# Eight weight-remainder subtractions moved from VectorE to GpSimd in a sparse-attention and feed-forward kernel

## The chip, the cores and the metric

The kernel runs on one core of one Trainium2 chip. A core has five engines with instruction queues of their own, which run in order: PE (TensorE, matrix products), DVE (VectorE), ACT (ScalarE), POOL (GpSimd) and SP (here it only issues transfers). The metric is the device time of one execution in microseconds, lower is better; the median of three runs stands for the kernel.

## The reference

Attention over 8 batches and 8 heads of 576 tokens with two kinds of masks, then a feed-forward layer over all 4608 tokens. Cut to what matters:

```python
scores = where(mask, q @ k.T / 8, -1e9)      # 4 heads local (32 back), 4 heads strided by 32
x = (softmax(scores) @ v)                    # then laid out as [4608, 512]
h = x @ w_in                                 # w_in  [512, 2048]
g = where(h >= 1, h, where(h <= -1, 0, (h + 1) ** 2 / 4))
out = g @ w_out                              # w_out [2048, 512]
```

The two weight matrices are given in double precision; everything else is single precision.

## The kernel before, in words

**Products.** Each single-precision factor is held as two parts in the matmul's input format `float32r`: a rounded high part and a low part, the remainder. A product is three matmuls (high by high, high by low, low by high; `HI_LO`). The last one of each three needs the low part of the weights.

**Chunks.** The 4608 tokens are cut in chunks of 512. Chunks 0 to 2 (`CLASSIC`) go through the feed-forward layer directly: for each of 16 blocks f of 128 hidden units, `up(c, f)` makes h (12 matmuls, line 775), the activation runs on ACT and DVE (lines 779, 782, 785), `rounded` splits it into `gh` and `gl` (lines 803 to 806), and two blocks later `down(c, f)` adds to the output (12 matmuls, line 820). The h tile of block f shares its bank with block f+2, so `up(c, f+2)` also waits for `gl` of block f. The remaining chunks use sums of weight blocks that POOL forms (`combine`, lines 396 and 398) and that go through DRAM.

**Weights.** In the first chunk the weights are not ready: block f arrives as raw 64-bit words, half 0 being `w_in` and half 1 `w_out`, and is turned into high and low parts while PE already works on the first blocks. A step is written as a letter, the block and the half, so `E4.0` is the low part of block 4's `w_in`:

- `A` (ACT, line 343) and `L` (ACT, line 347) scale the two 32-bit words of each number, `B` (DVE, line 351) shifts the high word, `C` (POOL, line 355) adds the two words. Now the number is single precision.
- `D` (ACT, line 364) rounds it to the high part, `E` (DVE, line 368) subtracts that from it and stores the low part. Both write the tile `w_f`.

`up(0, f)` needs `D` and `E` of half 0, `down(0, f)` those of half 1. When the last `E` of a block is done, its raw tile is free, and `stage()` loads another block into the place through SP's queue.

**Order.** All instructions stand in an order written out by hand: tables of numbers (`WORK`, `CONV`, ...) give each step a place on a common axis, on which a block of chunk 0 takes 4 units, from -64 to 0; the steps are sorted by that number, and each engine runs its own in that order. `CONV` holds the weight steps. Between them stand the steps of attention for the next batch: on POOL the subtraction of the row maximum (line 572) and the scaling by the row sum (line 596), on ACT the exponential (line 579), on DVE the masks, maxima and sums (lines 542, 568, 583). An engine that waits for one step's input holds up everything behind it in its queue.

Of the kernel before, what the change touches and what calls it, by code (L numbers as in the profile page):

```python
# [8 lines left out]
F32 = mybir.dt.float32  # L9
# [4 lines left out]
ALU = mybir.AluOpType  # L14
# [95 lines left out]
     (337.09, 3), (339.07, 6), (347.97, 4)]}  # L110

CONV = [(-63.99, 'L0.1'), (-63.97, 'A0.1 B0.1'), (-63.52, 'A1.1'), (-63.03, 'C0.1'), (-62.58, 'A3.0'), (-62.43, 'D0.1'),
# [28 lines left out]
G_WORK = {0: [(165.99, 's11'), (167.56, 's10'), (183.93, 's12'), (187.61, 's20'), (187.74, 's13'), (188.3, 't60'),  # L141
# [32 lines left out]
def tile_sparse_attention_then_ffn(  # L174
# [14 lines left out]
    nc = tc.nc  # L189
# [119 lines left out]
    def place(u, shape, dtype, name):  # L309
        return slot(f"w{u}", shape, dtype, name)  # L310
# [20 lines left out]
    def words(f, i):  # L331

        if i == 2:
            yield raws[f].rearrange("p i e t -> p (i e) t"), f in wt and wt[f].rearrange("p i h x e -> p (i h) x e")
            return
        for raw, e in pieces[f, i]:
            yield raw, f in wt and wt[f][:, i, e.start // HF:e.stop // HF]
# [19 lines left out]
    def whole(raw):  # L357
        return raw[:, :, 1].bitcast(F32).rearrange("p (h e) -> p h e", e=HF)

    def conv_d(f, i, copy=nc.scalar.copy):  # L360
        if f not in wt:
            wt[f] = place(f, [P, 2, 2, 2, HF], F32R, f"w_{f}")
        for raw, to in words(f, i):
            copy(to[:, :, 0], whole(raw))

    def conv_e(f, i):
        for raw, to in words(f, i):
            nc.vector.tensor_tensor(out=to[:, :, 1], in0=whole(raw), in1=to[:, :, 0].bitcast(F32), op=ALU.subtract)
        if i and f < len(PLACES):
            held.discard(PLACES[f])  # L370

# [2 lines left out]
    def stage(n=len(PLACES)):  # L374
        nonlocal staged
        while staged < n and ((staged, 0) in pieces or PLACES[staged] not in held):
            if (staged, 0) not in pieces:
                load_w(staged, 0)
            load_w(staged, 1)
            staged += 1  # L380
# [611 lines left out]
    def down_block(s, between):  # L992
        home = {"y": ("b0", "b1"), "x": ("b2", "b3"), "z": ("b4", "b5")}
        for n, (m, k) in enumerate(DOWN):
# [20 lines left out]


    conv = {"A": conv_a, "L": conv_l, "B": conv_b, "C": conv_c, "D": conv_d, "E": conv_e,
            "G": lambda f, i: conv_d(f, i, nc.vector.tensor_copy)}

    def begin(names):  # L1020
        for name in names.split():
# [6 lines left out]

    def conv_step(name):
        conv[name[0]](*map(int, name[1:].split(".")))  # L1030
        if name[0] == "E":
            stage()

    def last_weights(n):
# [8 lines left out]
    with tc.manual_schedule():  # L1043
# [33 lines left out]
        for s, work in G_WORK.items():  # L1077
            for t, name in work:
# [3 lines left out]
                agenda.append((t, 4, do, what))  # L1082
        agenda += [(t, 3, ship, (f, i)) for i, ts in enumerate(SHIP) for f, t in enumerate(ts)]
        agenda += [(t, 5, conv_step, (name,)) for t, names in CONV for name in names.split()]
        agenda.sort(key=lambda a: a[:2])

# [89 lines left out]
```

## Time and profile before

| | |
|---|---|
| median of 3 runs | 815.0 us (814.41, 815.0, 818.4) |
| profiled execution | 817.29 us, its span 815.5 us |
| granted TensorE clock | 1.00 |
| busy, share of the span | PE 99%, DVE 70%, ACT 61%, POOL 29% |

The span reaches from the first to the last instruction of the profiled execution; the 1.8 us between it and that execution's own time lie outside the program's instructions. Rows of the timeline give start and length in us, the engine, the line of the program, the operation, the tile written and those read, the shapes, how many like instructions were put together (`x2`), and in brackets how long the engine had been idle and what ended that. `fp32r` is the matmul input format. Instructions of one engine overlap by up to 0.1 us in the records, since one starts while the last still drains.

### The profile page before, as it was taken

To read this page: it belongs to the slowest core of one execution; us is meant where nothing else is said; L and a number is where in the kernel's file an instruction comes from. 1 tells how busy PE (TensorE), PEld (TensorE's weight loads), DVE (VectorE), ACT (ScalarE), POOL (GpSimd) and SP (SyncE) were. 2 spreads that over 40 slices of the span, in tenths; PEclk is the share of its full clock that TensorE was granted. 3 is DMA by queue.
4 is the path that set the end of the run, shared out by engine and by line. 5 is a ranking of instruction groups with operands and counts; after the bars stand their busy time and mean duration, and the time that the engine had idled before them with its cause. 6 is when DMAs were issued, how large, how long until landed. Compare 5 with 4: busy or idle time off the path is not lost.

```text
span 815.5 us, 17861 instructions
## 1 busy us (share of the span) xinstructions
PE 806.2 (99%) x6969; PEld 656.9 (81%) x6969; DVE 574.7 (70%) x850; ACT 495.4 (61%) x866; POOL 232.5 (29%) x226
## 2 busy tenths in 40 slices
PE   8999999999999999999999999999999999999998
PEld 6788888878878888887878888888888888888886
DVE  5898868767548477776778876675589834558664
ACT  5888955545355365776775453778654647775442
POOL 5353544873347543023222000220120001114100
PEclk9999999999999999999999999999999999999999
DMA  9936437788868867987998768887666776666765
GB/s 344 408 138 201 153 111 274 265 298 278 265 221 299 286 243 257 304 287 247 285 288 266 216 203 249 263 265 228 193 193 213 232 235 196 196 192 190 216 200 170
DMA packets 101796, 195.10 MB, mean 239 GB/s; under 512 B 17105, under 2 KB 32465, under 8 KB 99665
## 3 DMA queue, kind: packets, MB, share of 16 engines
q1 hardware_dynamic: 92496, 164.60, 63.3%
q10 hardware_dynamic: 9216, 29.36, 9.4%
q8 instruction: 55, 0.90, 0.5%
q14 instruction: 29, 0.23, 0.1%
HBM read 147.26 MB, written 46.66 MB: 238 GB/s over the span
## 4 chain that ended last, share of the span: by engine, by line
PE 91%; DMA 5%; issue 1%; DVE 1%; ACT 1%; POOL 0%; SPq 0%; ACTq 0%; POOLq 0%
PE o L820 16%; PE h L775 16%; PE yo L1005 15%; PE y L917 15%; PE zo L1005 8%; PE z L917 7%; PE xo L1005 4%; PE x L917 4%; PE xp L669 3%; PE sc L482 3%; DMA wr<-kq 1%; DMA qk<-in_qk_s 1%; DMA there<-t 1%; DMA pT<-there 1%; DMA qk<-in_qk_l 1%
## 5 line engine op out<-in xcount | busy, mean ns | idle before, releaser
L917 PE MATMUL y<-x,wr 128*128 128x512 f32 x576 | 141.3, 392 | 0.0
L775 PE MATMUL h<-xq,w 128*128 128x512 f32 x576 | 140.0, 392 | 0.1
L1005 PE MATMUL yo<-hl,wr 128*128 128x512 f32 x576 | 132.8, 390 | 0.6 <-DMA wr<-kq 0.6
L820 PE MATMUL o<-gh,w 128*128 128x512 f32 x384 | 130.1, 399 | 0.0
L1005 PEld LDWEIGHTS yo<-hl,wr 128*128 128x128 f32 x576 | 108.0, 188 | 23.4 <-DMA wr<-kq 1.0
L775 PEld LDWEIGHTS h<-xq,w 128*128 128x128 f32 x576 | 107.4, 188 | 23.4 <-DVE xq L739 0.7
L917 PEld LDWEIGHTS y<-x,wr 128*128 128x128 f32 x576 | 107.4, 188 | 22.7
L820 PEld LDWEIGHTS o<-gh,w 128*128 128x128 f32 x384 | 72.1, 188 | 16.2
L820 PE MATMUL o<-gl,w 128*128 128x512 f32 x192 | 75.0, 391 | 0.0
L917 PE MATMUL z<-x,wr 128*128 128x512 f32 x288 | 73.7, 391 | 0.0
L957 POOL TENSOR_TENSOR ga<-gb,ga 128x1024 f32<-128x1024 f32 x9 | 21.6, 2397 | 167.5 <-DVE ga L785 141.7
L1005 PE MATMUL zo<-hl,wr 128*128 128x512 f32 x288 | 66.1, 390 | 0.0
L572 POOL TENSOR_TENSOR pr<-pr,st 128x384 f32<-128x384 f32 (+3 forms) x21 | 26.3, 1253 | 135.7 <-DVE st L595 64.5
L1005 PEld LDWEIGHTS zo<-hl,wr 128*128 128x128 f32 x288 | 54.0, 188 | 11.3
L917 PEld LDWEIGHTS z<-x,wr 128*128 128x128 f32 x288 | 53.8, 188 | 11.3
L782 ACT ACTIVATE tmp<-tmp 128x512 f32<-128x512 f32 x96 | 60.7, 632 | 3.0
L871 DVE TENSOR_TENSOR hl<-ga,hl 128x1024 fp32r<-128x1024 f32 x36 | 47.3, 1315 | 19.9 <-ACT hl L870 18.2
L870 ACT CAST hl<-ga 128x1024 fp32r<-128x1024 f32 x36 | 38.0, 1056 | 35.1 <-PE yo L1005 12.6
L396 POOL TENSOR_TENSOR xs<-w 128x512 f32<-128x512 f32 x32 | 45.1, 1426 | 48.4 <-DMA ks<-xs 32.8
L785 DVE SCALAR_TENSOR_TENSOR h<-h,u 128x512 f32<-128x512 f32 x47 | 32.8, 697 | 30.5 <-ACT u L782 30.1
L398 POOL TENSOR_TENSOR xs<-xs 128x256 f32<-128x256 f32 x64 | 51.3, 802 | 5.0
L779 ACT ACTIVATE u<-h,half 128x512 f32<-128x512 f32 x48 | 33.1, 689 | 29.6 <-PE h L775 24.1
(120 smaller groups left out, 1321.9 us busy)
## 6 DMA issues: line engine op xcount, KB each, us to landing
wr<-ks SPq DMA_DIRECT2D x192, 256.0 KB, 3.9
wr<-kq SPq DMA_DIRECT2D x144, 256.0 KB, 3.4
ks<-xs ACTq DMA_DIRECT2D x16, 1024.0 KB, 4.8
raw<-in_w SPq DMA_DIRECT2D x30, 512.0 KB, 9.6
kq<-w ACTq DMA_DIRECT2D x48, 256.0 KB, 3.8
qk<-in_qk_s SPq DMA_DIRECT2D x16, 604.0 KB, 6.1
qk<-in_qk_l SPq DMA_DIRECT2D x16, 576.0 KB, 6.0
v<-in_v_l SPq DMA_DIRECT2D x21, 384.0 KB, 6.0
```

What stands on the lines that cost most here:

```text
L396: nc.gpsimd.tensor_tensor(out=b[:, :, f] if i else b[:, f], in0=hi, in1=lo, op=ALU.add)
L398: nc.gpsimd.tensor_tensor(out=st[:, to, HF:], in0=st[:, x, HF:], in1=st[:, y, HF:], op=op)
L572: eng.tensor_tensor(out=pr, in0=pr, in1=st[:, 0].unsqueeze(2).broadcast_to(list(pr.shape)), op=ALU.add)
L775: nc.tensor.matmul(o_ps[c, f], wt[f][:, 0, h, x, e:e + P], xq[c][:, y, cc], start=first and n == 0, stop=last and n == len(todo) - 1)
L779: nc.scalar.activation(u, h, AF.Relu, bias=half, scale=0.5)
L782: nc.scalar.activation(u, u, AF.Square)
L785: nc.vector.scalar_tensor_tensor(out=to, in0=h, scalar=1.0, in1=u, op0=ALU.max, op1=ALU.min)
L820: nc.tensor.matmul(o_ps[c][d], wt[f][:, 1, h, x, e:e + P], gs[y], start=f == 0 and n == 0, stop=f == NF - 1 and n == 2)
L870: nc.scalar.copy(t[:, 0], src)
L871: nc.vector.tensor_tensor(out=t[:, 1], in0=src, in1=t[:, 0].bitcast(F32), op=ALU.subtract)
L917: nc.tensor.matmul(to, w_[:, a, c * P:(c + 1) * P], xc[m][:, b, c], start=m in (1, 2, 5) and c + q == 0, stop=c == 1 and q == 2, skip_grou ...
L1005: nc.tensor.matmul(to, w_[jj][:, a, d * P:(d + 1) * P], t[:, b, jj], start=m in (1, 2, 5) and k + jj + q == 0, stop=k == NP // 2 - 1 and j ...
```

## The change

A new step letter `N` does what `E` does, with POOL's subtraction in place of DVE's. It stands in for `E` at the same numbers in half 1 (`w_out`) of the even blocks: `N0.1`, `N2.1`, ... `N14.1`, eight steps of one instruction each, 128x512 elements. Nothing else is moved.

```diff
- (-60.82, 'E0.1'), (-60.23, 'B1.1'), (-59.82, 'L3.0'), (-59.81, 'B3.0'), (-59.68, 'C3.0'), (-59.64, 'L1.1'),
+ (-60.82, 'N0.1'), (-60.23, 'B1.1'), (-59.82, 'L3.0'), (-59.81, 'B3.0'), (-59.68, 'C3.0'), (-59.64, 'L1.1'),
...
-    def conv_e(f, i):
+    def conv_e(f, i, eng=nc.vector):
         for raw, to in words(f, i):
-            nc.vector.tensor_tensor(out=to[:, :, 1], in0=whole(raw), in1=to[:, :, 0].bitcast(F32), op=ALU.subtract)
+            eng.tensor_tensor(out=to[:, :, 1], in0=whole(raw), in1=to[:, :, 0].bitcast(F32), op=ALU.subtract)
...
-            "G": lambda f, i: conv_d(f, i, nc.vector.tensor_copy)}
+            "G": lambda f, i: conv_d(f, i, nc.vector.tensor_copy),
+            "N": lambda f, i: conv_e(f, i, nc.gpsimd)}
...
-        if name[0] == "E":
+        if name[0] in "EN":
             stage()
```

In the rows below a tile's name ends in a running number, and the number before it is the block: `raw_3_209` is the raw tile of block 3, `w_2_660` the weights of block 2; `pr_1_0` are the scores of batch 1, unit 0.

POOL's queue at the first two moved steps (line 355 is `C`; the first `raw_0` row is `C0.1`, then come `C3.0`, `C1.1`, `C2.1`, `C4.0`):

```order
 L355 TENSOR_TENSOR raw_2_204<-raw_2_204 128x512
 L355 TENSOR_TENSOR raw_0_191<-raw_0_191 128x512
+L368 TENSOR_TENSOR w_0_516<-raw_0_191,w_0_516 128x2x256
 L355 TENSOR_TENSOR raw_3_209<-raw_3_209 128x512
 L355 TENSOR_TENSOR raw_1_198<-raw_1_198 128x512
 L355 TENSOR_TENSOR raw_2_204<-raw_2_204 128x512
+L368 TENSOR_TENSOR w_2_660<-raw_2_204,w_2_660 128x2x256
 L355 TENSOR_TENSOR raw_4_216<-raw_4_216 128x512
 L572 TENSOR_TENSOR pr_1_0_812<-pr_1_0_812,st_1_0_813 128x768
```

`C3.0` and `C4.0`, the additions for the `w_in` halves of blocks 3 and 4, now stand behind `N0.1` and `N2.1`, which wait for `D0.1` and `D2.1` on ACT.

DVE's queue at the first of them, between the split of block 0's activation and the shifts `B1.1` and `B3.0`:

```order
 L805 CAST gh_0_0_707<-u_0_0_699 128x512
 L806 TENSOR_TENSOR gl_0_0_708<-u_0_0_699,gh_0_0_707 128x512
-L368 TENSOR_TENSOR w_0_516<-raw_0_191,w_0_516 128x2x256
 L351 TENSOR_SCALAR raw_1_198<-raw_1_198 128x512
 L351 TENSOR_SCALAR raw_3_209<-raw_3_209 128x512
```

DVE goes from the split straight to the shifts, one instruction of line 368 fewer.

POOL's queue at the two moved steps of blocks 6 and 8:

```order
 L355 TENSOR_TENSOR raw_6_712<-raw_6_712 128x512
 L572 TENSOR_TENSOR pr_1_2_1098<-pr_1_2_1098,st_1_2_1099 128x12x54
+L368 TENSOR_TENSOR w_6_968<-raw_6_712,w_6_968 128x2x256
 L355 TENSOR_TENSOR raw_9_721<-raw_9_721 128x512
 L355 TENSOR_TENSOR raw_8_718<-raw_8_718 128x512
+L368 TENSOR_TENSOR w_8_1107<-raw_8_718,w_8_1107 128x2x256
 L355 TENSOR_TENSOR raw_9_721<-raw_9_721 128x512
```

Here the additions `C9.0` and `C9.1` come behind the moved steps.

14 rows, old and new, of the table CONV are left out of this document.

## The prediction

> **What bounds the kernel now.** I began with the page's busy line and the chain that ended last, then the busy time in ten-microsecond stretches, then PE's waits, and last the timeline of the 30 us in which PE runs just behind its weights.
>
> ```profile
> PE 806.2 (99%) x6969; PEld 656.9 (81%) x6969; DVE 574.7 (70%) x850; ACT 495.4 (61%) x866; POOL 232.5 (29%) x226
> ...
> PE 91%; DMA 5%; issue 1%; DVE 1%; ACT 1%; POOL 0%; SPq 0%; ACTq 0%; POOLq 0%
> ```
> ```profile
> core 0: us, PE busy (x) PEld busy (x) DVE busy (x) ACT busy (x) POOL busy (x), PEclk, DMA share, GB/s
> ...
> 40.00:50.00 10.00, 10.00 (x89) 8.04 (x71) 9.74 (x20) 9.12 (x18) 5.85 (x5) 1.00 0.78 312
> 50.00:60.00 10.00, 10.00 (x92) 8.15 (x91) 9.86 (x20) 8.59 (x16) 5.02 (x6) 1.00 0.01 2
> ```
> ```profile
> PE yo L1005 <- DMA wr<-kq: 0.6, 1, 0.6
> ```
> ```profile
> PEld h L775 <- DVE w L368: 0.3, 1, 0.3
> ```
>
> PE is busy 99% of the span and makes 91% of the last chain. From 30 us on PE's matrix rows show one wait, 0.6 us, far behind the change. So relief of another engine can win almost nothing, and any time that the change makes PE wait is added whole, since nothing behind it gives it back. But the second table shows that the margin is thin where the change sits: DVE is 97 to 99% busy from 40 to 60 us, ACT 86 to 91%, and the one weight load that waited for an `E` (0.3 us, last row) shows that PE is fed just in time there. POOL, half busy, looks as if it had room; yet what counts is which steps queue behind each `N` on POOL.
>
> **Prices.** DVE's rows around the first two moved steps, `E0.1` first, then `B1.1` with `B3.0`, `E4.0`, a row sum of attention and `E5.0`:
>
> ```profile
> 31.72 0.68 DVE L368 TENSOR_TENSOR w<-raw,w 128x512 fp32r<-128x512 f32 x1
> 32.33 0.76 DVE L351 TENSOR_SCALAR raw<-raw 128x512 uint32<-128x512 uint32 x2
> ...
> 42.04 0.68 DVE L368 TENSOR_TENSOR w<-raw,w 128x512 fp32r<-128x512 f32 x1
> ...
> 43.31 0.95 DVE L583 TENSOR_REDUCE st<-pr 128x12 f32<-128x768 f32 x1
> ...
> 48.63 0.63 DVE L368 TENSOR_TENSOR w<-raw,w 128x512 fp32r<-128x512 f32 x1
> ```
>
> What goes: eight DVE instructions of line 368 of 0.68 us. The next starts 0.61 us after the first of these rows, so about 0.6 us each, 4.8 us in all on DVE. What comes: eight POOL subtractions of 128x512 with two inputs in SBUF. POOL's nearest rows:
>
> ```profile
> 115.72 2.54 POOL L396 TENSOR_TENSOR xs<-w 128x512 f32<-128x512 f32 x2 [5.83 <-PE h L775]
> ```
> ```profile
> L957 POOL TENSOR_TENSOR ga<-gb,ga 128x1024 f32<-128x1024 f32 x9 | 21.6, 2397 | 167.5 <-DVE ga L785 141.7
> ```
> ```profile
> L355 POOL TENSOR_TENSOR raw<-raw 128x512 uint32<-128x512 uint32 x16 | 17.1, 1074 | 25.4 <-DVE raw L351 10.3 <-issue 4.8 <-DMA raw<-in_w 3.8
> ```
>
> The nearest is line 396: same engine, size, two inputs, the same weight tiles, 1.27 us each. The integer `C` (1.07 us) is the low end. No row of POOL writes `fp32r`; if that halves its rate, the high end is the 2.40 us of twice as many elements on line 957. I take 1.27.
>
> **One engine holds the other.** Two pairs of rows show that POOL and some DVE operations exclude each other:
>
> ```profile
> 48.86 1.73 POOL L596 TENSOR_TENSOR pr<-pr,st 128x768 f32<-128x768 f32 x1 [1.33 <-DVE st L595]
> 49.18 1.69 DVE L351 TENSOR_SCALAR raw<-raw 128x512 uint32<-128x512 uint32 x1
> ```
> ```profile
> 59.69 2.49 POOL L355 TENSOR_TENSOR raw<-raw 128x512 uint32<-128x512 uint32 x2 [1.37 <-ACT raw L347]
> ```
> ```profile
> 59.73 1.55 DVE L368 TENSOR_TENSOR w<-raw,w 128x512 fp32r<-128x512 f32 x1
> ```
>
> At 49.18 a `B`, of which two took 0.76 us above, takes 1.69 and ends 0.3 us after POOL's instruction (50.59); at 59.73 an `E`, above 0.68, takes 1.55 beside a `C`. So an `N` holds back any `B`, `E` or scaling (line 596) that DVE reaches meanwhile, up to 1.27 us. Operations that read a bank of PSUM are not held.
>
> The Trainium skill has this as a rule (SBUF — State Buffer, section Who interferes with whom): whichever of the two engines starts first keeps the shared port pair for its whole instruction, and the other blocks. By that rule, the trace agrees: the 1.69 us. Were the engines independent, `N0.1` would end at 32.9 us, before `C3.0` is due, and the sum below would be 0.4 us smaller in its first term and 0.6 smaller in the later ones, 1.4 us in place of 2.4.
>
> **The replay from 30 to 52 us.** With DVE's rows above, those of ACT, POOL and PE:
>
> ```profile
> 30.93 0.67 ACT L364 CAST w<-raw 128x512 fp32r<-128x512 f32 x1
> ...
> 34.45 0.66 ACT L364 CAST w<-raw 128x512 fp32r<-128x512 f32 x1
> ...
> 38.84 0.67 ACT L364 CAST w<-raw 128x512 fp32r<-128x512 f32 x1 [0.23 <-POOL raw L355]
> ...
> 40.54 0.68 ACT L364 CAST w<-raw 128x512 fp32r<-128x512 f32 x1
> ...
> 42.21 0.88 ACT L579 ACTIVATE pr<-pr 128x768 f32<-128x768 f32 x1
> ```
> ```profile
> 33.22 2.04 POOL L355 TENSOR_TENSOR raw<-raw 128x512 uint32<-128x512 uint32 x2 [3.23 <-DMA raw<-in_w]
> 37.76 2.04 POOL L355 TENSOR_TENSOR raw<-raw 128x512 uint32<-128x512 uint32 x2 [2.51 <-ACT raw L347]
> 40.34 1.79 POOL L572 TENSOR_TENSOR pr<-pr,st 128x768 f32<-128x768 f32 x1 [0.54 <-DMA raw<-in_w]
> ```
> ```profile
> 43.35 2.88 PE L775 MATMUL h<-xq,w 128*128 128x512 f32 x12
> ...
> 48.79 3.09 PE L775 MATMUL h<-xq,w 128*128 128x512 f32 x12
> ```
> ```profile
> 49.31 2.14 PEld L775 LDWEIGHTS h<-xq,w 128*128 128x128 f32 x10 [0.34 <-DVE w L368]
> ```
>
> *N0.1.* `D0.1` (30.93) ends at 31.60, `N0.1` runs from 31.65 to 32.9. `E0.1` (31.72) is gone, so `B1.1` and `B3.0` (32.33, 0.76 us together) come up at 31.72 and are held until 32.9, or go first and hold `N0.1`. Either way `N0.1` and both shifts are done at 33.6 to 33.75 and `C3.0` starts then, not at 33.22: +0.5. It ends at 34.75, and `D3.0` (34.45) starts at 34.85: +0.4, which ACT's queue and the shifts carry to `D2.1` (38.84), now at 39.25. PE doesn't wait yet.
>
> *N2.1.* It waits for `D2.1` to end at 39.9 and runs to 41.2. `C4.0`, the second of the pair at 37.76, so at 38.76 before, starts only then: +2.5, and ends at 42.3. Behind it on POOL the maximum's subtraction (40.34) runs from 42.3 to about 43.8. On ACT `D4.0` (40.54) goes to 42.35; it holds ACT's queue, the exponential (42.21) started 1.7 us after it with two steps between, so now at 44.05: +1.85. Its sum on DVE (43.31) follows at 45.1: +1.8. DVE is packed from there to `E5.0`, so that goes from 48.63 to 50.4 and ends at 51.05. PE's third weight load of `up(0,5)` already waited for it (49.31) and now gets it 1.8 us later. On the way `E4.0` (42.04), held by the subtraction on POOL until 43.8, ends at 44.5, and the third matmul of `up(0,4)`, due 0.46 us after 43.35, loses 0.7 us; that is part of the 1.8, as both are counted against the same clock. DVE's saved 0.6 us each of `E0.1` and `E2.1` win nothing: DVE waits for the `D`s, exponentials and shifts that now come later.
>
> The two steps together: **1.8 us**, 0.4 from `N0.1` and 1.4 from `N2.1`.
>
> **The other six.**
>
> ```profile
> 53.72 0.56 DVE L596 TENSOR_TENSOR pr<-pr,st 128x384 f32<-128x384 f32 x1
> ...
> 54.53 1.29 DVE L368 TENSOR_TENSOR w<-raw,w 128x512 fp32r<-128x512 f32 x2
> ...
> 71.85 0.68 DVE L368 TENSOR_TENSOR w<-raw,w 128x512 fp32r<-128x512 f32 x1
> ...
> 73.17 0.69 DVE L806 TENSOR_TENSOR gl<-h,gh 128x512 fp32r<-128x512 f32 x1
> ...
> 113.25 0.69 DVE L806 TENSOR_TENSOR gl<-h,gh 128x512 fp32r<-128x512 f32 x1
> ```
> ```profile
> 55.29 2.72 PE h L775 x12
> ...
> 74.81 2.72 PE h L775 x12
> ...
> 118.36 2.72 PE h L775 x12
> ```
>
> `N4.1` falls on the scaling at 53.72 and holds it some 0.7 us; `E6.0` is the first of the pair behind it (54.53, ended 55.2) and was needed 0.46 us after `up(0,6)` began at 55.3 or a little sooner: 0.4 to 0.5 us of room against 0.7. **0.3 us.** Then the missing `E4.1` gives DVE 0.6 back. `N6.1` holds `E8.0` about as long as the missing `E6.1` had taken: 0. `N8.1` falls on `E9.0` (71.85) and pushes it and the split of block 7 (73.17, ended 73.86) by up to 1.0 us, with 0.9 us of room to `up(0,9)` at 74.81, which shares the bank: **0.3 us** with the little that DVE is behind by then. `N10.1` and `N12.1` are of the same kind (at most 1.0 less the 0.6 saved), in a stretch where the load on DVE falls. `N14.1` holds the last two `C` by up to 2.7 us and through them ACT's queue, but block 14's split (ended 113.94) is needed at 118.36: 4.4 us of room. 0. Transfers of later blocks wait for a block's last `E`; `stage()` after `N6.1` issues 0.6 us later, after `N8.1` not later than before: 0.
>
> The sum is 1.8 + 0.3 + 0.3 = **2.4 us**. The profiled execution took 817.29 us with a span of 815.5 us, so it becomes 819.7 with a span of 817.9. The median of the runs is 2.3 us below that execution, and the same 2.4 us on it give **817.4 us**.
>
> **Rivals.**
>
> *Hidden.* If `N` costs 1.07 us and POOL and DVE happen to miss each other, `C4.0` is late by 1.9 instead of 2.5, and the packed stretch behind it takes some of that from the 1.2 us of DVE time saved ahead of it. Then PE waits 0 to 0.8 us: 815.0 to 815.8. The 0.34 us wait at 49.31 speaks against it: there is no room left at that place. Chance 0.25.
>
> *Slower, by a slow `fp32r` write on POOL.* If `N` takes 2.40 us as on line 957, the 1.13 us more are added at `N0.1`, `N2.1` and `N4.1`, each with the packed chain behind it: 2.4 + 3.4 = 5.8 us, 820.8 us. It decides from the point at which the three add 1.7 us, an `N` of 1.85 us. For it: no row of POOL writes that type. Against it: DVE writes it at the same 0.68 us as `f32`. Chance 0.18.
>
> *Faster, by DVE's relief.* 4.8 us leave an engine that is 98% busy around the place. But PE is the bound and shows only 0.3 us of waiting for `E`: 814.7 us at best, so over 0.5% (4.1 us) would need PE to wait in a way these rows don't show. Chance 0.04.
>
> That the change does nothing is excluded: the order shows eight instructions on another engine.
>
> **How the numbers follow.** My forecast, a loss of 0.8 to 4.1 us, has 0.53. A measurement of this kernel tells about 0.5% from no change, 4.1 us. The forecast and the hidden case lie within that: 0.78; slower 0.18; faster 0.04. The likeliest time is 817.4 us. The range starts at 814.6, the best of the hidden case with the 0.3 us gained, and ends at 820.2, within the slow case: about 0.1 is left out above and a little below.
>
> **What would show it.** Right: line 368 on POOL near 1.27 us; `C4.0` on POOL starting near 41.3; the exponential of 42.21 near 44; PE's loads of line 775 waiting for line 368 some 2 us in all between 43 and 58 us; nothing on PE after 80. Wrong: no PE wait there (hidden), or `N` rows of 1.85 us and more. Also wrong, if PE waits in a later place, such as block 14's bank, or if a transfer that starts after an `N` arrives late.

## Result and the profile after

| | before | after | ratio (95%) |
|---|---|---|---|
| median of 10 and 10 executions | 817.37 us | 821.79 us | 1.0054 (1.0036 to 1.0073) |
| the same kernels once more, 19 and 8 | 817.53 us | 820.85 us | 1.0042 (1.0026 to 1.0058) |
| profiled execution, its span | 817.29, 815.5 us | 820.3, 818.3 us | |

The change costs 3.3 to 4.4 us, 0.4 to 0.5%; the forecast was a loss of 2.4 us, 817.4 us. The page of the changed kernel begins:

```profile
PE 808.9 (99%) x6969; PEld 657.6 (80%) x6969; DVE 575.3 (70%) x842; ACT 496.6 (61%) x866; POOL 242.8 (30%) x234
```

DVE has eight instructions fewer and POOL eight more, as forecast. DVE's busy time isn't lower for it: other instructions got longer by what was saved. PE's waits from 30 us on, where before there was one of 0.6 us far behind the change (columns: us in total, times, longest):

```profile
PE h L775 <- DVE w L368: 1.1, 2, 0.6
PE h L775 <- DVE gl L806: 0.5, 1, 0.5
PE h L775 <- ACT raw L343: 0.3, 1, 0.3
PE xp L669 <- DMA pT<-there: 0.2, 1, 0.2
```

Two waits for an `E`, one for a `gl` (the bank shared with the block two before), one whose releaser is named from ACT, and one of 0.2 us for a transfer, far behind the change (between 400 and 600 us). To weigh such waits free of what happens before and behind, the measure from here on is the **stretch**: from PE's first matmul of `up(0,2)` to its first of `up(1,0)`. Its two ends before and then after, from the timeline (between those of before stand the starts of `up(0,6)` and `up(0,9)`):

```profile
31.37 0.50 PE L775 MATMUL h<-xq,w 128*128 128x512 f32 x1
...
55.13 2.88 PE L775 MATMUL h<-xq,w 128*128 128x512 f32 x12
...
74.65 1.52 PE L775 MATMUL h<-xq,w 128*128 128x512 f32 x6
...
118.20 1.07 PE L775 MATMUL h<-xq,w 128*128 128x512 f32 x4
```
```profile
32.56 0.72 PE L775 MATMUL h<-xq,w 128*128 128x512 f32 x2
...
122.69 1.52 PE L775 MATMUL h<-xq,w 128*128 128x512 f32 x6
```

That is 86.83 and 90.13 us: 3.30 us more. (All of this profiled execution is 1.19 us late already at 32.56, ahead of the first moved step, `N0.1`.) The places, from the starts of the `up` groups:

```profile
44.59 0.73 PE L775 MATMUL h<-xq,w 128*128 128x512 f32 x2
45.89 2.56 PE L775 MATMUL h<-xq,w 128*128 128x512 f32 x10 [0.57 <-DVE w L368]
...
51.45 0.70 PE L775 MATMUL h<-xq,w 128*128 128x512 f32 x2 [0.28 <-ACT raw L343]
52.64 2.60 PE L775 MATMUL h<-xq,w 128*128 128x512 f32 x10 [0.49 <-DVE w L368]
...
58.50 3.25 PE L775 MATMUL h<-xq,w 128*128 128x512 f32 x12
...
79.01 1.17 PE L775 MATMUL h<-xq,w 128*128 128x512 f32 x4 [0.46 <-DVE gl L806]
```

`up(0,4)` breaks after its second matmul (`E4.0` is late), `up(0,5)` starts late and breaks at the same point (`E5.0`): from `up(0,2)` to `up(0,6)` it is now 58.50 - 32.56 = 25.94 us, before 55.13 - 31.37 = 23.76: **+2.18**. `up(0,6)` takes 3.25 us in place of 2.88: **+0.38** to the next block. `up(0,9)` waits for its bank: **+0.74** with what follows it. Behind that nothing until `up(1,0)`. The late start of `up(0,5)` is another wait for the bank: it comes 0.15 us after the split of block 3 ended (DVE's row at 50.61 below), as that of `up(0,9)` comes 0.15 us after the split of block 7 (78.17); the row that names ACT is most likely this wait. It adds nothing to the loss, since `E5.0`, behind that split on DVE, comes later still.

POOL and then DVE at these places, both of the changed kernel:

```profile
32.88 1.32 POOL L368 TENSOR_TENSOR w<-raw,w 128x512 fp32r<-128x512 f32 x1 [1.73 <-DMA v<-in_v_l]
34.95 2.04 POOL L355 TENSOR_TENSOR raw<-raw 128x512 uint32<-128x512 uint32 x2 [0.76 <-ACT u L782]
39.71 1.04 POOL L355 TENSOR_TENSOR raw<-raw 128x512 uint32<-128x512 uint32 x1 [2.72 <-ACT u L779]
41.53 1.32 POOL L368 TENSOR_TENSOR w<-raw,w 128x512 fp32r<-128x512 f32 x1 [0.78 <-ACT w L364]
42.80 1.05 POOL L355 TENSOR_TENSOR raw<-raw 128x512 uint32<-128x512 uint32 x1
...
75.36 1.63 POOL L368 TENSOR_TENSOR w<-raw,w 128x512 fp32r<-128x512 f32 x1 [0.91 <-ACT w L364]
```
```profile
32.92 1.90 DVE L351 TENSOR_SCALAR raw<-raw 128x512 uint32<-128x512 uint32 x2
...
50.61 0.69 DVE L806 TENSOR_TENSOR gl<-h,gh 128x512 fp32r<-128x512 f32 x1
...
51.95 0.63 DVE L368 TENSOR_TENSOR w<-raw,w 128x512 fp32r<-128x512 f32 x1
...
57.04 1.16 DVE L596 TENSOR_TENSOR pr<-pr,st 128x384 f32<-128x384 f32 x1
...
69.56 2.32 DVE L368 TENSOR_TENSOR w<-raw,w 128x512 fp32r<-128x512 f32 x2
...
75.73 1.81 DVE L368 TENSOR_TENSOR w<-raw,w 128x512 fp32r<-128x512 f32 x1
78.17 0.69 DVE L806 TENSOR_TENSOR gl<-h,gh 128x512 fp32r<-128x512 f32 x1
```

`C4.0` (42.80) stands behind `N2.1` (41.53). Beside an `N`, DVE's shifts (32.92) take 1.90 us for 0.76, the scaling 1.16 for 0.56, the pair with `E8.0` (69.56) 2.32 where an unheld pair took 1.29 (54.53 before), and `E9.0` (75.73) 1.81 for 0.68. That is both mechanisms of the prediction. All eight `N`, by their line:

```profile
L368 POOL TENSOR_TENSOR w<-raw,w x8: 1307/1320/1631, 32.9 to 114.2; 128x512 fp32r<-128x512 f32 x8
```

The median is 1.32 us, against 1.27 taken.

### The profile page after: what moved, and what is told of

Read it like the earlier page. It is cut to its first block, busy times and chain, and to the rows that moved or that the text cites. A ratio compares the mean times of both kernels' runs of the same rounds, so it can differ in the third digit from the quotient of the medians.

```text
span 818.3 us, 17859 instructions
## 1 busy us (share of the span) xinstructions
PE 808.9 (99%) x6969; PEld 657.6 (80%) x6969; DVE 575.3 (70%) x842; ACT 496.6 (61%) x866; POOL 242.8 (30%) x234
## 4 chain that ended last, share of the span: by engine, by line
PE 88%; DMA 7%; DVE 2%; ACT 2%; issue 0%; POOL 0%; SPq 0%; DVEq 0%; POOLq 0%
PE yo L1005 16%; PE y L917 15%; PE o L820 14%; PE h L775 13%; PE zo L1005 8%; PE z L917 8%; PE xo L1005 4%; PE x L917 4%; DMA raw<-in_w 4%; PE xp L669 3%; PE sc L482 3%; DMA v<-in_v_l 1%; DMA pT<-there 1%; DMA there<-t 1%; DMA qk<-in_qk_l 1%; DVE w L368 1%
```

## The experiments

The theory was: the loss is PE waiting for weights, by the queue on POOL at `N0.1` and `N2.1` and by DVE held beside `N4.1` and `N8.1`. The rivals: one mechanism makes all of it; or the loss lies elsewhere (DMA, clock). All edits are made to the changed kernel; in the diffs `-` is the changed kernel. "E5.0" and "C4.0" in the table are starts against PE's start of `up(0,2)`, as differences from before; so are the next two columns. These four columns come from the one profiled execution of each kernel. Each ratio is against executions of before that ran beside that kernel (10, 17, 29 or 19 of them, medians 816.73 to 817.68 us).

| kernel | C4.0 | E5.0 | up(0,2) to up(0,6) | stretch | median, ratio (95%) |
|---|---|---|---|---|---|
| changed kernel | +2.85 | +2.13 | +2.18 | +3.30 | 821.79, 1.0054 (1.0036-1.0073) |
| the same again | +2.87 | +2.14 | +2.17 | +3.30 | 820.85, 1.0042 (1.0026-1.0058) |
| N0.1, N2.1 | +2.88 | +2.13 | +2.18 | +2.18 | 821.18, 1.0059 (1.0038-1.0079) |
| the other six | 0 | -0.04 | -0.04 | +1.11 | 819.53, 1.0035 (1.0022-1.0048) |
| N2.1 | +2.06 | +1.34 | +1.36 | +1.36 | 819.97, 1.0038 (1.0015-1.0061) |
| N2.1 behind C4.0 | +0.02 | +0.59 | +0.62 | +0.62 | 817.81, 1.0015 (1.0002-1.0028) |
| N0.1 | +0.75 | +0.73 | +0.74 | +0.75 | 818.22, 1.0005 (0.9989-1.0022) |
| fills in place of N | +1.89 | +1.16 | +1.16 | +1.16 | 818.41, 1.0006 (0.9986-1.0026) |
| DVE relieved | +0.81 | +0.33 | +0.34 | +0.34 | 817.33, 1.0000 (0.9984-1.0016) |
| N2.1 three times | +4.92 | +4.17 | +4.52 | +4.52 | 820.48, 1.0038 (1.0016-1.0060) |
| N2.1 six times | +9.03 | +8.33 | +8.40 | +8.59 | 825.67, 1.0092 (1.0075-1.0110) |
| N6.1, N10.1, N12.1, N14.1 | +0.03 | +0.02 | +0.05 | +0.05 | 818.28, 1.0011 (0.9995-1.0027) |

**The change in two halves.** First `N0.1` and `N2.1` alone, then the other six alone.

```diff
- 'N4.1' ... 'N14.1'      (six places)
+ 'E4.1' ... 'E14.1'
```

> Only N0.1 and N2.1 on GpSimd, the other six steps back on VectorE. I measure the stretch from PE's first matmul of up(0,2) to that of up(1,0): 86.83 us before, 90.13 with all eight (+3.30). Theory 1 (the additions C3.0 and C4.0 stand behind the moved steps on GpSimd, and the packed chain behind C4.0 makes PE wait for E4.0 and E5.0): most of it stays, +1.9 to +2.4 us. Rival (every moved step holds VectorE alike, 0.4 us each): +0.8 us. Rival (the loss is a reduced clock at the start, not the change): 0 in this stretch.

```diff
- 'N0.1' ... 'N2.1'
+ 'E0.1' ... 'E2.1'
```

> Only N4.1 to N14.1 on GpSimd, N0.1 and N2.1 back on VectorE. Theory 1: +0.2 to +0.9 us in the stretch, at up(0,6) and up(0,9), each where a moved step holds a VectorE instruction with little room behind it. Rival (alike for every step): +2.5 us. Rival (clock at the start): 0.

The stretches add up: 2.18 + 1.11 = 3.29, against 3.30 of all eight. The first half has its loss at `up(0,4)` and `up(0,5)` only; the second at `up(0,6)` (+0.43) and at `up(0,9)` with what follows it (+0.71), somewhat over the range. So there are two separate losses, and the larger one sits at `N0.1` and `N2.1`. The medians of these two runs stand 2.3 and 1.7 us higher above before than their stretches; more on that below.

**The queue taken apart.** `N2.1` alone, and `N2.1` alone but behind `C4.0` and the subtraction of the maximum (line 572) on POOL:

```diff
- (-60.82, 'N0.1') ... (-55.2, 'N2.1') ... 'N4.1' ... 'N14.1'
+ (-60.82, 'E0.1') ... (-55.2, 'N2.1') ... 'E4.1' ... 'E14.1'
```

> N2.1 alone at its place. Theory 1: C4.0 starts about 2.1 us later than 38.76 us, up(0,4) and up(0,5) wait, +1.2 to +1.7 us in the stretch. Rival (alike for every step): +0.4 us. Rival (clock): 0.

```diff
- (-60.82, 'N0.1') ... (-55.2, 'N2.1') ... 'N4.1' ... 'N14.1'
+ (-60.82, 'E0.1') ... (-52.4, 'N2.1') ... 'E4.1' ... 'E14.1'
```

> N2.1 alone, but behind C4.0 and the maximum's subtraction on GpSimd and ahead of C5.0; it still ends before down(0,2) needs it. If only the place in GpSimd's queue counts: 0 to +0.2 us in the stretch. If the holding of VectorE counts as well (theory 1 has both): up(0,4) no longer waits, but B5.0 and B3.1 are held until about 43.5 us and E5.0 comes 0.5 to 1.0 us late: +0.5 to +1.0 us, all of it at up(0,5).

Behind `C4.0` the step costs 0.62 us in place of 1.36. So 0.74 us go with its place in the queue, but not all. In the later place, POOL first, then DVE, then PE:

```profile
42.09 1.77 POOL L368 TENSOR_TENSOR w<-raw,w 128x512 fp32r<-128x512 f32 x1
```
```profile
42.60 1.88 DVE L351 TENSOR_SCALAR raw<-raw 128x512 uint32<-128x512 uint32 x2
```
```profile
50.21 0.96 PE L775 MATMUL h<-xq,w 128*128 128x512 f32 x3 [0.47 <-DVE w L368]
```

The shifts `B5.0` and `B3.1` are held (1.88 us for two that took 0.76 before), and DVE, packed from there to `E5.0`, carries it to PE. Neither of the two places tried for `N2.1` is free of cost: in front of `C4.0` it holds the queue, behind it it holds DVE.

`N0.1` alone:

```diff
- (-55.2, 'N2.1') ... 'N4.1' ... 'N14.1'
+ (-55.2, 'E2.1') ... 'E4.1' ... 'E14.1'
```

> N0.1 alone on GpSimd. The prediction has 0.4 us for it. The two runs that held N0.1 and N2.1 together and N2.1 alone differ by 2.18 - 1.36 = 0.82 us in the stretch. If N0.1 has its own price whatever follows, the stretch from up(0,2) to up(1,0) grows by 0.7 to 0.9 us to 87.5 to 87.7; if it is dear only because N2.1 stands behind it (its delay of C3.0 pushes D2.1, for which N2.1 waits), by 0.2 to 0.5 us.

It costs 0.75 us by itself, not the 0.4 of the prediction; with `N2.1`'s 1.36 that makes 2.11 of the 2.18. In its queues `C3.0` is 0.53 us late, `D3.0` 0.37 and the shift `B2.1` 0.40, as forecast; but `C2.1` is 0.75 late. DVE, then POOL:

```profile
38.80 0.76 DVE L351 TENSOR_SCALAR raw<-raw 128x512 uint32<-128x512 uint32 x2
39.47 1.02 DVE L542 TENSOR_TENSOR pr<-sc,m_loc 128x384 f32<-128x384 f32 x2
```
```profile
40.04 2.04 POOL L355 TENSOR_TENSOR raw<-raw 128x512 uint32<-128x512 uint32 x2 [2.73 <-DMA raw<-in_w]
```

Before, this pair (`C2.1`, `C4.0`) started 0.13 us after the end of the shift, while the mask's addition (line 542) ran. Here the shifts end at 39.56 and it starts at 40.04, the moment the first of the two additions ends. It is the same in the changed kernel (39.71 against 39.15 + 0.55) and in the runs with `N0.1` and `N2.1` and with DVE relieved. The trace names a different releaser nearly each time; why these 0.35 us are lost in the one group of runs and not in the other stays open.

The first part of this loss is the hold, not the queue, as the prediction had it and the theory above had not: in the changed kernel `N0.1` ends at 34.20 (32.88 + 1.32), the held shifts at 34.82 (32.92 + 1.90), and `C3.0` starts at 34.95, right behind the shifts. So of the four places only `N2.1`, 1.36 us, is the queue's.

**Which part is the hold.** Each `N` replaced on POOL by two fills, the first waiting for `D` as `N` does; the first overwrites the raw word already used, the second puts zeros in the low part. These eight low parts are left out of the result.

```diff
-            eng.tensor_tensor(out=to[:, :, 1], in0=whole(raw), in1=to[:, :, 0].bitcast(F32), op=ALU.subtract)
+            if eng is nc.vector:
+                eng.tensor_tensor(...)
+            else:
+                eng.memset(raw[:, :, 1], 0)
+                eng.memset(to[:, :, 1].bitcast(F32), 0.0)
```

> All eight N are in place, but each is replaced on GpSimd by two fills of the same size that read nothing: one of the used raw word, behind the wait for D as before, and one of the low part with zeros, which leaves these eight low parts out of the result. The question is which part of the loss is the queue on GpSimd and which is VectorE held while the two-input subtraction runs. If the queue (C4.0 behind the wait for D2.1, then the length of the step) makes the loss at up(0,4) and up(0,5), it stays within about 0.5 us of the 2.1 us of the changed kernel as long as the two fills together take 0.8 us or more; VectorE's instructions beside a fill keep their own lengths (B1.1 0.4 us, the scaling of line 596 0.56, E8.0 and E9.0 0.65 to 0.68), and the loss at up(0,6) (0.38 us) and up(0,9) (0.74 us) goes: PE's stretch from up(0,2) to up(1,0) 88.5 to 89.0 us, 1.7 to 2.2 more than before. If a fill holds VectorE like the subtraction, all four places stay: 89.6 to 90.2 us. If the hold was the cause at up(0,4) and up(0,5) as well, 87.2 us or less.

Three of POOL's fills and what DVE ran beside them:

```profile
31.24 0.57 POOL L371 MEMSET raw<- 128x512 uint32 x1 [1.72 <-ACT w L364]
...
54.32 0.53 POOL L372 MEMSET w<- 128x512 f32 x1
...
72.19 0.59 POOL L371 MEMSET raw<- 128x512 uint32 x1 [1.62 <-ACT w L364]
```
```profile
31.29 1.58 DVE L351 TENSOR_SCALAR raw<-raw 128x512 uint32<-128x512 uint32 x2
...
54.42 0.56 DVE L600 TENSOR_TENSOR pr<-pr,st 128x384 f32<-128x384 f32 x1
...
72.19 0.68 DVE L369 TENSOR_TENSOR w<-raw,w 128x512 fp32r<-128x512 f32 x1
```

The scaling and `E9.0` run beside a fill at their own lengths, and the losses at `up(0,6)` and `up(0,9)` are gone: those two were the hold of two-input DVE instructions by a POOL instruction that reads; a fill, which only writes, leaves them alone. The shifts, though, are held by a fill as well (1.58 us for 0.76), against my expectation. The Trainium skill (SBUF — State Buffer, section Who interferes with whom) makes just this difference: a two-input DVE instruction contends with a GpSimd one that reads, not with one that only writes, while a `tensor_scalar`, which can run in a two-port mode, contends with GpSimd in that mode without such an exception. By that rule, the trace agrees: 0.56 and 0.68 against 1.58 us. The loss that is left is 1.16 us, under the 1.7 to 2.2 expected: the two fills take 1.03 us in place of 1.32, and `C2.1` is only 0.11 us late here, as its shift is. It is nearly all the queue's: `C4.0` is 1.89 us late, the 2.06 of `N2.1` alone less the 0.29 by which the fills are shorter, and 0.12 from the held shifts.

**DVE's relief alone.** One fill of the low part, not waiting for `D`, in place of each `N` (the same low parts are left out):

```diff
-            eng.tensor_tensor(out=to[:, :, 1], in0=whole(raw), in1=to[:, :, 0].bitcast(F32), op=ALU.subtract)
+            if eng is nc.vector:
+                eng.tensor_tensor(...)
+            else:
+                eng.memset(to[:, :, 1].bitcast(F32), 0.0)
```

> The eight steps on VectorE are gone, and nothing that waits for D is put on GpSimd: one fill of the low part with zeros stands there instead, ready long before (it leaves these eight low parts out of the result). This is VectorE's relief nearly alone. As PE showed 0.3 us of waiting for VectorE in this stretch, the stretch from up(0,2) to up(1,0) should be 86.5 to 86.9 us, 0 to 0.3 less than before, and the time the same as before within 0.2%. The rival, that VectorE's 4.8 us are worth something that the change only hid, wants 1 us less or more. If the clock of TensorE is lowered by PE's new stalls, it stays here at the loss of before: (1 - clock) x 817 us of 0.6 us or less in the mean, against 2.1 us in the changed kernel.

The time is that of before (ratio 1.0000), and the stretch is 0.34 us longer, not shorter. `C2.1` loses its 0.35 us here too, and `D2.1` and `D4.0` behind it on ACT are 0.35 and 0.36 us late; the fill of 0.5 us ahead of `C4.0` goes into the slack ahead of `D4.0`. The mean of (1 - clock) x 817 us is 0.9 us, not the 0.6 expected, and 1.0 in the 29 executions of before beside it. PE's one wait in the stretch is still for `E5.0`:

```profile
PE h L778 <- DVE w L369: 0.3, 1, 0.3
```

Eight subtractions fewer on an engine that is 98% busy bring nothing here: DVE then waits twice for ACT (0.2 and 0.3 us), and `E5.0` comes no earlier.

**The four at no cost.** Only the four that the prediction put at 0:

```diff
- 'N0.1', 'N2.1', 'N4.1', 'N8.1'
+ 'E0.1', 'E2.1', 'E4.1', 'E8.1'
```

> Only N6.1, N10.1, N12.1 and N14.1 on GpSimd, the four that the prediction put at 0. If that is right, the stretch from up(0,2) to up(1,0) is that of before, 86.8 us within 0.15, and the time within 0.2% of before; the 1.11 us of the six late steps then belong to N4.1 and N8.1 alone. If their hold on VectorE or the transfers behind their later loads cost something, 0.3 us or more show in the stretch or behind it.

The stretch is 86.88 us, 0.05 more than before, and the ratio's interval includes 1, though `E8.0` is held as in the changed kernel:

```profile
67.49 2.32 DVE L368 TENSOR_TENSOR w<-raw,w 128x512 fp32r<-128x512 f32 x2
```

So a hold alone costs nothing where DVE is not about to be waited for, and the 1.11 us belong to `N4.1` and `N8.1`.

**Length and clock.** After the first runs the medians seemed to rise by more than the stretches, and the executions with the moved steps showed lower granted clocks: (1 - clock) x 817 us, what the granted clock falls short of full speed, was 2.1 us in the mean for the changed kernel, 0.6 for 17 executions of before. Two runs with a longer `N2.1`, and the changed kernel again, were to show whether PE's new waits pull the clock down.

```diff
-            eng.tensor_tensor(out=to[:, :, 1], in0=whole(raw), in1=to[:, :, 0].bitcast(F32), op=ALU.subtract)
+            for _ in range(1 if eng is nc.vector else 3):
+                eng.tensor_tensor(out=to[:, :, 1], in0=whole(raw), in1=to[:, :, 0].bitcast(F32), op=ALU.subtract)
```

(with `N2.1` as the only `N`; the second kernel has 6 for 3)

> N2.1 alone on GpSimd, its subtraction written three times, so the step takes 3.9 us in place of 1.3. If its length passes one for one through the queue, PE's stretch from up(0,2) to up(1,0) grows from 88.19 us (N2.1 once) by 2.6 us to 90.8, with PE's stalls at up(0,4) and up(0,5) together near 4 us. On the clock: if TensorE's stalls themselves make the throttle grant half speed for stretches of 3.41 us behind them, such stretches now show in the profiled execution between 43 and 62 us, the mean of (1 - clock) x 817 us rises above the 2.45 us of N2.1 once to 3 us or more, and the median grows by more than the stretch, to 823 us or more. If the lower clocks of the changed kernel were chance or came from before 31 us, the loss stays near 0.6 to 2 us and the median is near 820.5.

> N2.1 alone on GpSimd with its subtraction written six times (about 7.9 us for the step). By the rule that the runs so far follow, E5.0 and with it PE come later by the delay of C4.0 less 0.72 us: C4.0 + 8.6 us, E5.0 + 7.9, the stretch 94.7 us where no grant is lowered. With three subtractions a stall of 2.5 us in 3.41 us was followed by one stretch of 3.41 us at half clock. Here PE stands for more than one such stretch, so two at half clock or more are expected between 43 and 66 us, the stretch is 95 to 97 us, and hardly an execution has a clock of 0.998 or more. If the grants do not follow the stalls, one or none is seen there and clocks of 1.0 still occur.

Busy time in windows (columns: window, its length, then each engine's busy time with its count, the granted clock, DMA share and GB/s); three times first, then six times:

```profile
40.70:44.10 3.40, 2.76 (x12) 1.90 (x11) 0.79 (x2) 0.00 (x0) 3.24 (x4) 1.00 1.03 408
44.10:47.50 3.40, 1.53 (x5) 0.97 (x6) 2.11 (x4) 2.80 (x5) 2.38 (x3) 1.00 0.92 369
47.50:50.90 3.40, 3.40 (x9) 2.63 (x8) 3.04 (x8) 2.68 (x6) 1.81 (x3) 0.50 0.08 31
50.90:54.30 3.40, 3.40 (x16) 2.77 (x15) 3.37 (x6) 3.37 (x7) 2.04 (x2) 1.00 0.00 0
```
```profile
45.30:48.70 3.40, 0.00 (x0) 0.00 (x0) 0.00 (x0) 0.00 (x0) 3.16 (x4) 1.00 0.64 258
48.70:52.10 3.40, 0.80 (x2) 0.50 (x2) 0.82 (x1) 1.51 (x3) 3.29 (x3) 0.50 0.00 0
52.10:55.50 3.40, 3.33 (x8) 2.35 (x8) 3.12 (x8) 2.72 (x6) 2.09 (x2) 0.50 0.00 0
55.50:59.00 3.50, 3.50 (x17) 2.89 (x16) 3.39 (x9) 3.50 (x7) 0.91 (x2) 1.00 0.00 0
```

On the length: two more subtractions make `C4.0` 2.86 and `E5.0` 2.83 us later, and three more again 4.11 and 4.16. So the step's length passes one for one to PE once the slack is used up. (The stretch of three times is 0.35 us longer than its `E5.0` is late; PE ran at half clock just there.)

On the clock: in these two executions a window of 3.4 us in which PE stood for more than half of it is followed by one at half clock, and two such windows by two. The clocks of all four executions of six times are 0.996 or less, as two windows at half clock would give. Three times is less clear: its median is 820.48 us, not 823 or more, its mean clock loss 2.1 us, not 3 or more, and one of its eight executions has a clock of 1.0. So a wait of some 2 us can lower the clock, but doesn't each time. The changed kernel's waits are shorter: in no 3.4 us of its stretch do its matmul records leave more than 0.76 us free.

> The changed kernel once more, for its median and its clocks. Its PE stretch from up(0,2) to up(1,0) was 3.30 us longer than before, its median 4.4 us. If the stretch is the whole loss and the rest scatter, the median now lies 2.6 to 4.0 us over that of before, and the mean of (1 - clock) x 817 us within 0.7 us of that of before. If PE's new stalls of up to 0.75 us in 3.41 us also lower the granted clock in some executions, that mean stays near the 2.1 us of the first ten executions, 1 us or more above before, the median 4 us or more above it, and a profiled execution may show a grant of 0.5 between 42 and 62 us.

The median is 3.3 us above before, the mean clock loss 1.2 us against 1.2 us of the 19 executions of before beside it, and in neither of the two profiled executions of the changed kernel does a lowered grant stand between 30 us and the end of PE's work. The four at no cost had a mean clock loss of 1.7 us with no new wait of PE. So for the changed kernel the stretch is the loss, and the clock is not shown to add to it. Medians follow the stretches only roughly: those of the two halves and of `N2.1` alone lie 1.7 to 2.3 us higher above before than their stretches, that of `N2.1` three times 1.7 us lower, the others within 1.1. This is left open; in the first three the mean clock loss was 2.1, 1.6 and 2.5 us against 0.6 of before beside them, which would fit in size, but that of `N2.1` three times was above before too (2.1 against 1.0), and its median is the one that lies lower.

## Why the prediction was wrong

The sign and both mechanisms held; the number came out too low by its base and by three terms. Of the 4.4 us between the forecast of 817.4 and the measured 821.79 us, 2.4 are the base (817.37 against 815.0), 0.9 the terms (a stretch 3.30 us longer, against 2.4 forecast), and 1.1 lie outside the stretch; these did not come back when the kernels ran again (820.85 against 817.53, a loss of 3.3).

- **The base.** The sum of 2.4 us was put on the median of three, 815.0 us, though the profiled execution it was worked out from took 817.29. Over 10, 17, 29 and 19 executions the medians of before are 817.37, 816.73, 817.68 and 817.53. Against the profiled execution the sum gave 819.7; the two profiled executions of the changed kernel took 820.3 and 819.91 us. The three were a low draw, and the choice between 815.0 and 817.29 was worth nearly as much as the whole loss that was forecast. The failed step is the sentence that puts the same 2.4 us on the median of the runs.
- **`N0.1`: 0.4 forecast, 0.75 measured.** The failed step is "which ACT's queue and the shifts carry to `D2.1` (38.84), now at 39.25": against `up(0,2)` it is 39.59, since `C2.1` lost another 0.35 us beyond the 0.40 of its shift. Up to there each step held: `C3.0` forecast at +0.5, measured +0.55, `D3.0` +0.4 and +0.39. Why `C2.1` lost the 0.35 stays open.
- **`N2.1`: 1.4 forecast, 1.36 measured.** `C4.0` alone 2.06 late; both steps together make 2.85 against 2.5 forecast, which is the same 0.35. `C4.0` to PE: the forecast lets 0.7 of the delay disappear in ACT's slack ahead of `D4.0`; the table shows 0.70 to 0.75 in every run in which `N2.1` or the two fills stand in front of `C4.0`. That `up(0,5)` would also wait for its bank, shared with block 3, the prediction did not have; it costs nothing on top.
- **`N4.1`: 0.3 forecast, 0.38 measured** (0.43 with the six alone). The scaling was held by 0.60 us, forecast 0.7.
- **`N8.1`: 0.3 forecast, 0.74 measured.** The step "by up to 1.0 us, with 0.9 us of room" had both numbers wrong: the hold on `E9.0` is 1.13 us (1.81 - 0.68), the split of block 7 ends 1.25 us later against `up(0,8)`, and `up(0,9)` began at 74.65, not 74.81, in the matmul's own rows; `up(0,9)` now starts 0.15 us after the split, so the room was 0.64. 1.25 - 0.64 is the wait of 0.61; 0.13 more follow in the next block.
- **The four at 0** hold: 0.05 us together.
- **Price of an `N`:** 1.27 taken, 1.32 measured. The rival of a slow `fp32r` write falls; so do the relief of DVE (relief alone: ratio 1.0000) and the hidden case, since PE does wait.
- The signs named in advance: `C4.0` near 41.3 (41.61 by PE's clock), the exponential near 44 (44.38), PE's loads waiting some 2 us for line 368 (1.9 from 43 to 58 us, 2.4 with `up(0,6)`), all seen; "nothing on PE after 80" held for the weights, with the last such wait at 79.01, and the only later one is the 0.2 us for a transfer.

No version that beats both kernels follows from this: before, PE's only wait in the stretch is 0.3 us for `E5.0`, and the intervals here reach 1 us and more to either side.

## What to carry to other kernels

When an engine is fed just in time, an instruction moved to another engine's queue costs what stands behind it there: trace the delay to the next consumer that PE waits for, subtract the slack once, and expect the rest in full. POOL work beside a packed DVE is charged twice, in POOL's queue (1.36 us here, at `N2.1`) and in DVE's held instructions (where `N0.1`, `N4.1` and `N8.1`, 1.87 us together, have their start), so such a move is free only where neither has a near deadline, as with four of the eight here. Make the sum against the execution whose rows it uses, and don't move it to a median of three whose spread is larger than the effect.

## What the runs showed of the hardware beyond that

- PE's clock was halved for 3.41 us after a window, taken to end where the lower clock begins, in which PE was still busy for 1.53 of 3.40 us (`N2.1` three times). The Trainium skill (TensorE: Matmul & The Clock Gate, section Part 1: The HAM clock gate) speaks of an idle window of about 3.4 us before the clock falls; here the window need not be idle throughout. Some executions had one such window also before 31 us, after a window with PE busy for 2.53 of 3.40 us, as the changed kernel's first:

```profile
15.70:19.10 3.40, 2.53 (x100) 2.04 (x101) 2.40 (x8) 3.12 (x9) 2.96 (x3) 1.00 1.02 407
19.10:22.50 3.40, 3.40 (x57) 3.33 (x58) 2.48 (x7) 2.01 (x6) 2.23 (x3) 0.51 1.03 417
```

  How much must be free can't be read from these traces: in the run with `N0.1` and `N2.1` PE was busy for 2.02 of 3.40 us from 19.98 us, and no lower clock followed. What such a window costs shows at the first matmul of `up(0,2)`: 32.6 to 33.1 us in the five profiled executions that had one before 31 us, 30.9 to 31.8 in the eight that had none. That would explain the 1.19 us by which the changed kernel's first was late there.

- An `N` can itself be longer beside DVE: 1.63 us at 75.36 and 1.77 in the later place, against 1.32.
